# State-exchange attention feeding a gated two-layer network on one core: x first, the first layer's first step in plain float32, a new TensorE order in batch 0, and batch 1's second softmax moved behind it

## The chip, the core and the metric

The kernel runs on one core of one Trainium2 chip. The metric is the device time of one execution in microseconds (us), the median of the runs. TensorE (PE) multiplies matrices into PSUM, VectorE (DVE) and ScalarE (ACT) work element by element, SyncE (SP) issues most of the DMA transfers, and GpSimd (POOL) does almost nothing here. TensorE's weight loads are shown by the profile as an engine of their own, PEld.

## The reference

There are 8 batches `b` of 8 heads, 512 tokens and 32 states of 64 numbers. Token scores are turned into two softmaxes, one over the states for every token and one over the tokens for every state:

```python
scores = scale * x @ state.T          # a  = softmax over the 32 states
xread  = a @ state                    # 512 tokens read from the states
scores2 = scale * state @ x.T         # a2 = softmax over the 512 tokens
sread  = a2 @ x                       # 32 states read from the tokens
y = concat([xread, sread])            # 544 rows per head; heads side by side: 512 columns
h = y @ w_in                          # 512 -> 2048
g = where(h >= 1, h, where(h <= -1, 0, (h + 1)**2 / 4))
out = g @ w_out                       # 2048 -> 512
```

The weights come in as float64. They reach the kernel as pairs of 32-bit words, 1 MB for each of 16 chunks: 8 of `w_in` (256 of the 2048 columns each) and 8 of `w_out`.

## The kernel before

**The products.** The kernel doesn't form `xread`. It multiplies the states with each chunk of `w_in` (`sw_product`, L403, the tile `sw`) and then the softmax with that, which gives `h` directly (`Hidden.product`, L464). A number is split into a float32r part that is rounded (`...h`) and the rest (`...l`), and a product is three float32r matmuls: high by high, low by high, high by low (L478 to L480, and L538 to L540 for the second layer, `g2`). The scores, `sw`, the transposes on TensorE (`e2p`, `rt`) and the read of the states (`sr`) are plain float32.

**A step.** For each batch and each `j` of 0 to 7 there is one step of layer one (`g1`: two banks `h` of 128x512, 12 float32r matmuls), then the gate (`relu`, `square` on ACT, `bound` on DVE), the split of its result into `gh` (ACT, L500) and `gl` (DVE, L505), and one step of layer two (`g2`: 24 float32r matmuls into four banks `acc`). A bank `h` is read by `relu` and once more by `bound`, and is free after that. There are two banks `h`, four `acc`, and one pair of banks for transient results, `mm`, which `sw`, `e2p`, `sr`, `rt` and the scores of batches 1 to 7 share in turn. Batch 8 holds the state rows of all batches.

**Batch 0.** While batch 0 is computed the weights arrive and are made from their words: `high` (ACT, L592), `low` (ACT L584 or DVE L579), `join` (DVE, L600, into `w32` for `w_in`, into `wf` for `w_out`), and for `w_out` the split `part_high` (ACT, L607) and `part_low` (DVE, L611). The raw words of `w_in` have two buffers; SP issues the load of chunk `c + 2` when `w32` of chunk `c` is joined, and loads that stand behind it in SP's queue wait too.

**What sets the order.** All of batch 0 is recorded as operations with an engine, a cost, what they need and which buffers they take (`Plan`, L23). On TensorE and SP the order is that in which they are recorded; on DVE and ACT a list schedule puts the operation with the longest tail first, shifted by the numbers in `BIAS`. `emit` also fills TensorE's planned idle time before the first `g2` with multiplications of an identity matrix (`warm`, L195, tile `warmed`), whose results nobody reads. From batch 1 on the order is written out (`attention`, L803, and the loop at L840).

**Names.** `turn`, `top1`, `less1`, `exp1`, `sum1`, `inv1`, `norm1`, `back`, `high1`, `rest` make the first softmax `z`, its transpose `zt` and the split `ath`, `atl`. `top2`, `exp2` make the second softmax `e2`; `turn2` and `keep_turned` transpose it on TensorE and copy it back, or `turn_blocks` (DVE) and `shuffle` (16 DMAs on SP) do so without TensorE; `read2`, `scale2`, `keep2`, `keep` make the rows `srT`.

Of the kernel before, what the change touches and what calls it, by code (L numbers as in the profile page):

```python
# [17 lines left out]
WARM = 10  # L18
PAD = 120
BIAS = {('square', 0, 7): 4.9, ('high', 'o', 5): 4.6, ('wol', 7): -5.5, ('back', 0, 1): 2.8, ('atl', 1, 0): -6.5, ('w', 1): -2.8, ('swh', 0, 4): 4.5, ('wol', 5): 9.6, ('top2', 1, 1): 2.5, ('woh', 5): 4.1, ('swl', 1, 0): -0.5, ('swl', 0, 7): 2.1, ('gh', 0, 7): 0.6, ('low', 'i', 0): 2.6, ('wol', 6): 4.0, ('back', 1, 0): -2.1, ('turn', 0, 0, 1): -8.6, ('bound', 1, 0, 0): 3.3, ('high', 'o', 0): -4.3}  # L20
# [117 lines left out]
def state_exchange_moe(  # L138
# [68 lines left out]
    wo = {}  # L207
# [17 lines left out]
    class Attention:  # L225
# [60 lines left out]
        def inv1(self, q):  # L286
            _, _, s = self.parts(q)
# [14 lines left out]
        def high1(self, q):  # L302
            nc.scalar.copy(out=self.ath[:, q], in_=self.zt[:, q])
# [99 lines left out]
    def sw_product(b, c, n, apart=False):  # L403

        if apart:
            banks = [ps_h(f"sw{b}_{c}_{hh}") for hh in range(2)]
# [11 lines left out]
        w = n * CI  # L418
        wh, wl = (
# [36 lines left out]
    class Hidden:  # L456


        def __init__(self, b, j):
            self.b, self.j = b, j  # L460
            self.u = work.tile([P, 2, S], F32, tag="u", bufs=1, name=f"u{b}_{j}")
# [20 lines left out]

        def relu(self, i):
# [12 lines left out]
        def high(self):  # L496
# [3 lines left out]
            nc.scalar.copy(out=gh, in_=self.u)  # L500
# [18 lines left out]
    def g2(b, j, half=None):  # L519
# [12 lines left out]
        for i, t in pairs:  # L532
# [3 lines left out]
            lh, ll = (v[:, i // per, c0:c0 + P] for v in (gh, gl))  # L536
            a = acc[b][t]
            nc.tensor.matmul(a, lhsT=lh, rhs=oh, start=f == 0, stop=False)  # L538
# [55 lines left out]
    def join(kind, c):  # L594
# [3 lines left out]
        else:  # L598
            a = parts[c] = work.tile([P, 1024], F32, tag="tmp", name=f"wf{c}")
# [5 lines left out]
    def part_high(c):  # L605
        wo[c] = wop.tile([P, 2, 2, DM], F32R, tag="wo", name=f"wo{c}")
        nc.scalar.copy(out=wo[c][:, 0].rearrange("p a c -> p (a c)"), in_=parts[c])  # L607
# [17 lines left out]
    def chunk_ops(c):  # L625
# [24 lines left out]
    def att_ops1(b):  # L650
        def m(name, *a):
            return lambda: getattr(atts[b], name)(*a)

        for q in range(2):
# [14 lines left out]
            op(("inv1",) + k, "DVE", 0.4, m("inv1", q), [("sum1",) + k])  # L669
            op(("norm1",) + k, "DVE", 0.62, m("norm1", q), [("inv1",) + k])  # L670
        for q in range(2):
# [3 lines left out]
            op(("ath",) + k, "ACT", 0.52, m("high1", q), [("back",) + k], ends=[("zt", b)])  # L675
            op(("atl",) + k, "DVE", 0.62, m("rest", q), [("ath",) + k], ends=[("zt", b)])

    def att_ops2(b):
        def m(name, *a):
            return lambda: getattr(atts[b], name)(*a)  # L680

        for q in range(2):
            k = (b, q)
            take = [("tmp" if b == 0 else "e2", ("e2", b))] if q == 0 else []
            op(("top2",) + k, "DVE", 0.75, m("top2", q), [("sc", b) if b else ("sc", b, 1)] + [("top2", b, 0)] * q, take=take)
            op(("exp2",) + k, "ACT", 0.66, m("exp2", q), [("top2",) + k], ends=[("sc", b)])
        op(("kept", b), "ACT", 0.95, m("keep_turned"), [("e2p", b)], ends=[("e2p", b)])
# [3 lines left out]
    hid = {}  # L691

    def hidden_ops(b, j):
        k = (b, j)
        for i in range(2):
            op(("relu", i) + k, "ACT", 0.58, lambda i=i: hid[k].relu(i), [("p", i) + k], ends=[("h", i) + k],
               take=[("u", ("u",) + k)] if i == 0 else [])
# [3 lines left out]
        op(("gh",) + k, "ACT", 0.97, lambda: hid[k].high(), [("bound", 0) + k, ("bound", 1) + k],  # L701
# [6 lines left out]
    def product(i, b, j):  # L708
        if i == 0:
            hid[b, j] = Hidden(b, j)  # L710
        hid[b, j].product(i)

    def sw_ops(b, c, n):
        tensor(("sw", b, c), 0.35 + 0.35 * n, lambda: sw_product(b, c, n), [("w", c + i) for i in range(n)],
# [188 lines left out]
```

## Time and profile before

| | |
|---|---|
| time, median of 3 runs | 655.29 us (654.06 to 3663.21) |
| time of the profiled execution | 655.34 us |
| its span, first to last instruction | 653.6 us |
| PE busy | 644.3 us, 99% of the span |
| DVE busy, ACT busy | 354.7 us (54%), 371.5 us (57%) |
| mean granted TensorE clock | 0.997 |
| DMA | 46.80 MB, 72 GB/s over the span |
| second `h` step of batch 0 starts | 27.94 us |
| first `h` step of batch 1 starts | 99.60 us |

The time of an execution is 1.7 us more than its span. A row of the trace's timeline gives the start, the busy time, engine, line, operation, `out<-in`, the shape and how many instructions were merged; in brackets stands the idle time before it and what ended it. Busy times of neighbours overlap a little, so how long an instruction holds its engine is read from start to start.

### The profile page before, as it was taken

The numbers are of one execution on the slowest core, as the hardware profiler recorded it, in microseconds if no ns is written. First come the engines' busy times: TensorE is split into PE (matmuls) and PEld (weight loads), VectorE is DVE, ScalarE is ACT, GpSimd is POOL, SyncE is SP. The second block draws the span as 40 slices with busy tenths as digits, with TensorE's granted clock in tenths as the row PEclk, the third lists the DMA queues.
The fourth block names the chain that finished last, engine by engine and source line by source line (L and its number), as shares of the span: only waits on it lengthen the run. The fifth ranks groups of instructions, "written<-read, shape, count | busy, mean of one in ns | idle before, by whom it ended". The sixth has DMA issues, their size and how long they took to land.

```text
span 653.6 us, 10398 instructions
## 1 busy us (share of the span) xinstructions
PE 644.3 (99%) x4396; PEld 514.7 (79%) x4396; DVE 354.7 (54%) x514; ACT 371.5 (57%) x529; POOL 0.8 (0%) x7
## 2 busy tenths in 40 slices
PE   7999999999999999999999999999999999999997
PEld 6777777788777877787877877787877878788896
DVE  4999954564446643664456534664356543335531
ACT  4899856554546545655645555555545464545641
POOL 0000000000000000000000000000000000000000
PEclk9899999999999999999999999999999999999999
DMA  8897201032101401041101401031102001000101
GB/s 351 342 396 294 66 1 64 1 73 90 49 18 20 143 1 64 2 97 66 65 1 29 133 1 64 10 89 65 65 0 35 1 5 61 2 1 0 65 1 32
DMA packets 37198, 46.80 MB, mean 72 GB/s; under 512 B 27424, under 2 KB 27552, under 8 KB 34080
## 3 DMA queue, kind: packets, MB, share of 16 engines
q1 hardware_dynamic: 36672, 45.30, 20.1%
q10 hardware_dynamic: 480, 0.85, 0.4%
q8 instruction: 34, 0.56, 0.4%
q14 instruction: 12, 0.10, 0.1%
HBM read 34.08 MB, written 8.91 MB: 66 GB/s over the span
## 4 chain that ended last, share of the span: by engine, by line
PE 92%; ACT 4%; DVE 2%; DMA 1%; issue 0%; ACTq 0%; SPq 0%
PE acc L538 19%; PE acc L539 18%; PE acc L540 18%; PE h L478 10%; PE h L480 10%; PE h L479 10%; PE sw L414 4%; DMA xt<-in_xt_dram 1%; PE sr L369 1%; PE sc L253 1%; PE warmed L198 1%; ACT u L484 1%; ACT raw_i L592 1%; ACT gh L500 0%; ACT raw_o L592 0%; ACT u L488 0%
## 5 line engine op out<-in xcount | busy, mean ns | idle before, releaser
L538 PE MATMUL acc<-wo,gh 128*128 128x512 f32 x544 | 214.9, 395 | 0.0
L539 PE MATMUL acc<-wo,gh 128*128 128x512 f32 x544 | 212.2, 390 | 0.0
L540 PE MATMUL acc<-wo,gl 128*128 128x512 f32 x544 | 211.8, 389 | 0.0
L491 DVE SCALAR_TENSOR_TENSOR u<-u,h 128x512 f32<-128x512 f32 x136 | 92.8, 687 | 191.5 <-ACT u L488 191.5
L484 ACT ACTIVATE u<-h,half 128x512 f32<-128x512 f32 x136 | 93.7, 690 | 154.9 <-PE h L480 153.8
L538 PEld LDWEIGHTS acc<-wo,gh 128*128 128x128 f32 x544 | 102.1, 188 | 29.9 <-issue 8.7
L505 DVE TENSOR_TENSOR gl<-u,gh 128x1024 fp32r<-128x1024 f32 x68 | 83.2, 1224 | 68.2 <-ACT gh L500 68.1
L540 PEld LDWEIGHTS acc<-wo,gl 128*128 128x128 f32 x544 | 102.1, 188 | 21.8
L539 PEld LDWEIGHTS acc<-wo,gh 128*128 128x128 f32 x544 | 102.2, 188 | 20.4
L500 ACT CAST gh<-u 128x1024 fp32r<-128x1024 f32 x68 | 71.4, 1050 | 47.6 <-DVE u L491 47.6
L488 ACT ACTIVATE u<-u 128x512 f32<-128x512 f32 (+1 forms) x128 | 84.5, 660 | 3.8
L414 PE MATMUL sw<-w,sb 64*32 64x256 f32 x1024 | 33.1, 381 | 2.2 <-DVE w L600 2.2
L414 PEld LDWEIGHTS sw<-w,sb 64*32 64x32 f32 x1024 | 17.7, 106 | 14.3 <-issue 6.7
L478 PE MATMUL h<-ath,sw_6h 128*128 128x512 f32 x60 | 24.6, 410 | 0.0
L553 ACT COPY o<-acc 128x512 f32<-128x512 f32 x33 | 18.0, 587 | 10.9 <-PE acc L540 10.9
L478 PE MATMUL h<-ath,sw_2h 128*128 128x512 f32 x60 | 24.1, 402 | 0.0
L478 PE MATMUL h<-ath,sw_0h 128*128 128x512 f32 x60 | 23.6, 393 | 0.0
L480 PE MATMUL h<-atl,sw_2h 128*128 128x512 f32 x60 | 23.4, 391 | 0.0
L479 PE MATMUL h<-ath,sw_6l 128*128 128x512 f32 x60 | 23.4, 390 | 0.0
L480 PE MATMUL h<-atl,sw_6h 128*128 128x512 f32 x60 | 23.4, 390 | 0.0
L479 PE MATMUL h<-ath,sw_0l 128*128 128x512 f32 x60 | 23.4, 389 | 0.0
L480 PE MATMUL h<-atl,sw_0h 128*128 128x512 f32 x60 | 23.4, 389 | 0.0
(176 smaller groups left out, 726.3 us busy)
## 6 DMA issues: line engine op xcount, KB each, us to landing
raw_i<-in_moe_w_in_dram SPq DMA_DIRECT2D x8, 1024.0 KB, 6.3
raw_o<-in_moe_w_out_dram SPq DMA_DIRECT2D x8, 1024.0 KB, 8.7
xn<-in_x_dram SPq DMA_DIRECT2D x8, 1024.0 KB, 5.2
out_dram<-o SPq DMA_DIRECT2D x32, 256.0 KB, 2.2
xt<-in_xt_dram SPq DMA_DIRECT2D x15, 512.0 KB, 4.7
e<-eb SPq DMA_DIRECT2D x96, 32.0 KB, 1.9
xt<-in_xt_dram ACTq DMA_DIRECT2D x1, 512.0 KB, 7.6
sb<-in_state_dram SPq DMA_DIRECT2D x1, 448.0 KB, 11.8
```

What stands on the lines that cost most here:

```text
L414: nc.tensor.matmul(banks[hh][pr * NS:(pr + 1) * NS, i * CI:(i + 1) * CI], lhsT=sb[rows, b, pr], rhs=w32[c + i][rows, pr], start=True, stop ...
L478: nc.tensor.matmul(o, lhsT=wh[:, k, sl], rhs=ah[:, k], start=first, stop=False)
L479: nc.tensor.matmul(o, lhsT=wl[:, k, sl], rhs=ah[:, k], start=False, stop=False)
L480: nc.tensor.matmul(o, lhsT=wh[:, k, sl], rhs=al[:, k], start=False, stop=last)
L484: nc.scalar.activation(out=self.u[:, i], in_=self.hs[i], func=AF.Relu, scale=0.5, bias=half)
L488: nc.scalar.activation(out=u, in_=u, func=AF.Square)
L491: nc.vector.scalar_tensor_tensor(out=self.u[:, i], in0=self.u[:, i], scalar=1.0, in1=self.hs[i], op0=ALU.min, op1=ALU.max,)
L500: nc.scalar.copy(out=gh, in_=self.u)
L505: nc.vector.tensor_tensor(out=gl, in0=self.u, in1=gh.bitcast(F32), op=ALU.subtract)
L538: nc.tensor.matmul(a, lhsT=lh, rhs=oh, start=f == 0, stop=False)
L539: nc.tensor.matmul(a, lhsT=lh, rhs=ol, start=False, stop=False)
L540: nc.tensor.matmul(a, lhsT=ll, rhs=oh, start=False, stop=f == NF - 1)
```

## The change

- **Loads.** Both halves of batch 0's `x` are issued by SP, ahead of the weights; before, ACT issued the second half. ACT loads its function table with a one-element `Exp` at the start.
- **First scores.** Batch 0's scores go into the pair of banks `mm` instead of two banks `acc`. `sw` of chunks 0 and 1 goes into banks `acc` (the letter `a` in `ORDER`).
- **First step of layer one.** With `NH = 1`, step 0 of batch 0 isn't split: `sw` of chunk 0 is copied whole (`wh`, float32), and `product_part` multiplies it with the whole `zt`: four plain float32 matmuls of 128x512 in place of twelve float32r ones. `NG = 0`, so the code for a layer two in plain float32 (`part_late`, the branches on `NG`) is not used.
- **TensorE's order in batch 0** is written as words in `ORDER`. `sw3.2` and `sw5.2` make two chunks at once. The halves of `g2` stand in another order.
- **Batch 1's second softmax** is transposed by DVE and DMAs, as in later batches, and its `read2`, `scale2`, `keep2` and `keep` stand in batch 1, after its steps 1 and 3. The load of `xn` for batch 2 goes behind them.
- **Smaller things.** `inv1` is done for both halves at once; `WARM` is 6, not 10; the planner has other costs, other numbers in `BIAS`, and a table `ENG` that puts some copies on DVE and some `low` on ACT.

```diff
-WARM = 10
+WARM = 6
+NH = 1
+NG = 0
+ENG = {('low', 'o', 1): 'ACT', ('low', 'o', 2): 'ACT', ('woh', 5): 'DVE', ('low', 'o', 5): 'DVE', ('ath', 0, 0): 'DVE', ('low', 'i', 5): 'ACT', ('low', 'o', 3): 'ACT', ('woh', 3): 'DVE'}
+ORDER = "sw0.1a h0 sw1.1a e2p h1 sw2.1 g0.0 sr h2 g0.1 sw3.2 g1.0 h3 sc1 g2.1 g2.0 rt h4 g1.1 sw5.2 g3.1 g3.0 h5 sw7.1 g4.0 h6 g4.1 g5.1 h7 g5.0 g6.0 g6.1"
...
-            (nc.scalar if i and b == 0 else nc.sync).dma_start(out=xt[:, i], in_=xt_in[b, i])
+            nc.sync.dma_start(out=xt[:, i], in_=xt_in[b, i])
...
-                if b:
-                    sc = ps_mm(f"sc{b}")
-                    self.sc = [sc[:, hh] for hh in range(2)]
-                else:
-                    self.sc = [ps_acc(f"sc{b}_{hh}") for hh in range(2)]
+                sc = ps_mm(f"sc{b}")
+                self.sc = [sc[:, hh] for hh in range(2)]
...
-    def sw_product(b, c, n, apart=False):
+    def sw_product(b, c, n, apart=None):
...
-            banks = [ps_h(f"sw{b}_{c}_{hh}") for hh in range(2)]
+            banks = [apart(f"sw{b}_{c}_{hh}") for hh in range(2)]
...
+        if b == 0 and c < NH:
+            whole = work.tile([P, 1024], F32, tag="wh", name=f"sw{b}_{c}w").rearrange("p (q f) -> p q f", q=2)[:, :, :w]
+            sw_of[b, c] = [(banks[q][:, :w], whole[:, q], None) for q in range(2)]
+            chunk[b, c] = whole, None
+            return
...
+        def product_part(self, k):
+
+            j = self.j
+            if k == 0:
+                self.hs = [ps_h(f"h0_{j}_{i}") for i in range(2)]
+            w, _ = chunk[0, j]
+            for i in range(2):
+                nc.tensor.matmul(
+                    self.hs[i], lhsT=w[:, k, i * P:(i + 1) * P], rhs=atts[0].zt[:, k], start=k == 0, stop=k == 1
+                )
...
+        if b:
+            for q in range(2):
+                op(("blocks", b, q), "DVE", 0.62, m("turn_blocks", q), [("exp2", b, q)] + [("blocks", b, 0)] * q,
+                   take=[("tmp", ("eb", b))] if q == 0 else [])
+            return
...
     nc.scalar.dma_start(out=sb[:, 0], in_=state[:, 0])
+    nc.scalar.activation(out=small.tile([P, 1], F32, name="tabled"), in_=half, func=AF.Exp)
...
+    read(("eb", 1), 2.0, lambda: atts[1].shuffle(), after=[("blocks", 1, 0), ("blocks", 1, 1)])
...
+    for name in ("read2", "scale2"):
+        later("mid", 1, 1, (lambda name=name: getattr(atts[1], name)(),))
+    later("mid", 1, 1, (load_later, 2))
+    for name in ("keep2", "keep"):
+        later("mid", 1, 3, (lambda name=name: getattr(atts[1], name)(),))
```

The order of the instructions shows two places. The first is VectorE in batch 0, from the second transpose `back` of the first softmax to the first `bound` of step 0. Before (`z`, `zt` the softmax, `wf_247` and `wo_260` chunk 0 of `w_out`, `raw_i_178` and `raw_o_223` the words of chunk 2 of `w_in` and chunk 1 of `w_out`):

```order
L300 STREAM_TRANSPOSE zt_176<-z_117 128x512
L306 TENSOR_TENSOR atl_114<-zt_176,ath_113 128x512
L436 TENSOR_TENSOR sw_0l<-sw_0_205,sw_0h 128x512
L306 TENSOR_TENSOR atl_114<-zt_176,ath_113 128x512
L600 SCALAR_TENSOR_TENSOR w_1_88<-raw_i_128 128x1024
L600 SCALAR_TENSOR_TENSOR wf_247<-raw_o_145 128x1024
L579 TENSOR_SCALAR raw_i_178<-raw_i_178 128x1024
L611 TENSOR_TENSOR wo_260<-wf_247,wo_260 128x1024
L436 TENSOR_TENSOR sw_1l<-sw_1_263,sw_1h 128x512
L579 TENSOR_SCALAR raw_o_223<-raw_o_223 128x1024
L491 SCALAR_TENSOR_TENSOR u_0_239<-u_0_239,h_0_1_252 128x512
```

The same stretch of VectorE in the changed kernel (`wf_248` is chunk 0 of `w_out`, `raw_i_197` the words of chunk 2 of `w_in`):

```order
L301 STREAM_TRANSPOSE zt_205<-z_114 128x512
L318 TENSOR_REDUCE nm_0_193<-sc_113 128x1
L319 TENSOR_SCALAR nm_0_193<-nm_0_193 128x1
L662 CAST ath_111<-zt_205 128x512
L307 TENSOR_TENSOR atl_112<-zt_205,ath_111 128x512 x2
L627 SCALAR_TENSOR_TENSOR wf_248<-raw_o_142 128x1024
L602 TENSOR_SCALAR raw_i_197<-raw_i_197 128x1024
L441 TENSOR_TENSOR sw_1l<-sw_1_0_235,sw_1h 128x256
L441 TENSOR_TENSOR sw_1l<-sw_1_1_236,sw_1h 128x256
L511 SCALAR_TENSOR_TENSOR u_0_214<-u_0_214,h_0_0_215 128x512
```

The rest of `sw` of chunk 0, the split of chunk 0 of `w_out` (L611 before) and the `low` of chunk 1 of `w_out` have left the stretch. One cast of `ath` has come in, and the join of `w_1` and the second `top2` (L318, L319) have changed sides: the join now stands ahead of the second `back`, `top2` behind it. Further up, one `low` (chunk 0 of `w_in`) has come to VectorE from ScalarE.

The second place is TensorE from the end of step 0 to the start of step 1 of layer one. Before:

```order
L480 MATMUL h_0_1_252<-atl_114,sw_0h 128x512
L414 MATMUL sw_1_263<-w_1_88,sb 32x256 x8
L198 MATMUL warmed<-ident 128x128 x4
L333 MATMUL e2p_285<-ident,e_0_153 128x128 x8
L198 MATMUL warmed<-ident 128x128
L478 MATMUL h_1_0_304<-ath_113,sw_1h 128x512
L479 MATMUL h_1_0_304<-ath_113,sw_1l 128x512
L480 MATMUL h_1_0_304<-atl_114,sw_1h 128x512
```

The same in the changed kernel, from the last two of the eight multiplications of `sw_1`:

```order
L414 MATMUL sw_1_0_235<-w_1_88,sb 32x256
L414 MATMUL sw_1_1_236<-w_1_88,sb 32x256
L333 MATMUL e2p_250<-ident,e_0_192 128x128 x8
L202 MATMUL warmed<-ident 128x128 x6
L487 MATMUL h_1_0_277<-ath_111,sw_1h 128x512
L488 MATMUL h_1_0_277<-ath_111,sw_1l 128x512
L489 MATMUL h_1_0_277<-atl_112,sw_1h 128x512
```

`sw_1` has two tiles of its own, in banks `acc`, so `e2p` no longer takes the banks that `sw_1` had, and the multiplications by the identity stand behind `e2p`.

More of the change, by code (lines that the diff above doesn't have):

```diff
@@ L494, in bound, with high @@
             )
-        def high(self):
+        def high(self, engine="ACT"):
             b, j = self.b, self.j
@@ L535, in g2 @@
             c0 = (i % per) * n + t * P
-            lh, ll = (v[:, i // per, c0:c0 + P] for v in (gh, gl))
+            lh, ll = (v if v is None else v[:, i // per, c0:c0 + P] for v in (gh, gl))
             a = acc[b][t]
+            if ll is None:
+                nc.tensor.matmul(a, lhsT=lh, rhs=ol, start=f == 0, stop=False)
+                continue
             nc.tensor.matmul(a, lhsT=lh, rhs=oh, start=f == 0, stop=False)
@@ L691, in state_exchange_moe @@
     hid = {}
+    made = {}
     def hidden_ops(b, j):
         k = (b, j)
+        whole = b == 0 and j < NG
         for i in range(2):
-            op(("relu", i) + k, "ACT", 0.58, lambda i=i: hid[k].relu(i), [("p", i) + k], ends=[("h", i) + k],
-               take=[("u", ("u",) + k)] if i == 0 else [])
+            op(("relu", i) + k, "ACT", 0.58, lambda i=i: hid[k].relu(i), [("p", 1 if j < NH else i) + k], ends=[("h", i) + k],
+               take=[(("g", ("g",) + k) if whole else ("u", ("u",) + k))] if i == 0 else [])
         op(("square",) + k, "ACT", 0.97, lambda: hid[k].square(), [("relu", 0) + k, ("relu", 1) + k])
@@ L710, in product, with sw_ops @@
             hid[b, j] = Hidden(b, j)
[L711 to L716 removed]
+        if b == 0 and j < NH:
+            hid[b, j].product_part(i)
+        else:
+            hid[b, j].product(i)
+    def sw_ops(b, c, n, kind=""):
+        for i in range(n):
+            made[b, c + i] = c
+        tensor(("sw", b, c), 0.35 + 0.35 * n, lambda: sw_product(b, c, n, ps_acc if kind else None),
+               [("w", c + i) for i in range(n)],
+               take=[("acc" if kind else "mm", ("sw", b, c)), ("w", ("wc", b, c))])
+        flex(("swh", b, c), "ACT", (0.5 * n, 0.6 * n), lambda e: sw_high(b, c, e), [("sw", b, c)], ends=[("sw", b, c)])
+        if b == 0 and c < NH:
+            return
         op(("swl", b, c), "DVE", 0.6 * n, lambda: sw_low(b, c), [("swh", b, c)], ends=[("sw", b, c)])
@@ L720, in g1_ops @@
         for i in range(2):
-            need = [(x, b, j) for x in ("swh", "swl")] + [(x, b, q) for x in ("ath", "atl") for q in range(2)]
+            if j < NH:
+                need = [("swh", b, j), ("back", b, i)]
+                tensor(("p", i, b, j), 1.75, lambda i=i: product(i, b, j), need,
+                       take=[("h", ("h", x, b, j)) for x in range(2)] if i == 0 else [], ends=[("wc", b, j), ("zt", b)])
+                continue
+            need = [(x, b, made[b, j]) for x in ("swh", "swl")] + [(x, b, q) for x in ("ath", "atl") for q in range(2)]
             tensor(("p", i, b, j), 1.4, lambda i=i: product(i, b, j), need, take=[("h", ("h", i, b, j))],
-                   ends=[("wc", b, j)])
+                   ends=[("wc", b, made[b, j])])
     def g2_ops(b, j, half):
         k = (b, j)
-        tensor(("g2", half) + k, 2.75, lambda: g2(b, j, half), [("gh",) + k, ("gl",) + k, ("wol", j), ("sc done", 0)],
+        need = [("bound", 0) + k, ("bound", 1) + k, ("join", j)] + [(x, 0, c) for x, c in (("swh", 0), ("swh", 1), ("swl", 1)) if (x, 0, c) in plan.ops] if j < NG else [("gh",) + k, ("gl",) + k, ("wol", j)]
+        tensor(("g2", half) + k, 3.5 if j < NG else 2.75, lambda: g2(b, j, half), need,
                ends=[("g",) + k])
@@ L772, in state_exchange_moe @@
[L772 to L785 removed]
+        "e2p": lambda: tensor(("e2p", 0), 0.9, lambda: atts[0].turn2(), [("exp2", 0, 0), ("exp2", 0, 1)],
+                              take=[("mm", ("e2p", 0))]),
@@ new lines, in state_exchange_moe @@
+        "sr": lambda: tensor(("sr", 0), 1.1, lambda: atts[0].read2(), [("kept", 0), ("dma", "xn", 0)],
+                             take=[("mm", ("sr", 0))], ends=[("e2", 0), ("xn", 0)]),
+        "sc1": lambda: tensor(("sc", 1), 1.1, lambda: att_start(1), [("dma", "sb", 1), ("dma", "xt", 1)],
+                              take=[("mm", ("sc", 1))], ends=[("xt", 1)]),
+        "rt": lambda: tensor(("rt", 0), 0.3, lambda: atts[0].keep2(), [("rs", 0)], take=[("mm", ("rt", 0))]),
+    }
+    for word in ORDER.split():
+        if word in between:
+            between[word]()
+            if word == "sc1":
+                att_ops1(1)
+                att_ops2(1)
+        elif word[0] == "s":
+            c, n = word[2:].split(".")
+            sw_ops(0, int(c), int(n[0]), n[1:])
+        elif word[0] == "h":
+            g1_ops(0, int(word[1]))
+            hidden_ops(0, int(word[1]))
+        else:
+            g2_ops(0, int(word[1]), int(word[3]))
@@ L830, in state_exchange_moe @@
     later("end", 1, 0, (sw_make, 1, (2,)))
+    for c in range(NG):
+        later("mid", 1, 0, (part_late, c))
     later("mid", B - 1, 6, (states_split,))
```

127 lines of the change are left out of this document (65 added, 62 removed).

## The prediction

> **What bounds the kernel now.** I read the page first, then busy time by stretches, then TensorE's waits.
>
> ```profile
> PE 644.3 (99%) x4396; PEld 514.7 (79%) x4396; DVE 354.7 (54%) x514; ACT 371.5 (57%) x529; POOL 0.8 (0%) x7
> ```
>
> ```profile
> 0.00:31.50 31.50, 26.40 (x212) 21.42 (x212) 22.12 (x43) 20.14 (x26) 0.83 (x7) 0.95 0.88 353
> 31.50:100.00 68.50, 68.36 (x528) 51.30 (x521) 58.06 (x79) 55.54 (x71) 0.00 (x0) 1.00 0.47 184
> 100.00:200.00 100.00, 100.00 (x658) 78.70 (x658) 52.27 (x77) 56.56 (x86) 0.00 (x0) 1.00 0.15 48
> ```
>
> ```profile
> PE sw L414 <- DVE w L600: 2.2, 1, 2.2
> PE sc L253 <- DMA xt<-in_xt_dram: 1.0, 1, 1.0
> PE e2p L333 <- DVE sw_1l L436: 0.5, 1, 0.5
> ```
>
> The columns of the stretches are length, then busy time of PE, PEld, DVE, ACT, POOL, the clock, DMA share and GB/s. TensorE is never idle from 31.5 us on, and its only idle spells lie ahead of that. So the time is the moment at which TensorE begins gapless work, plus that work. What TensorE does before is in the timeline of its first 28 us:
>
> ```profile
> 1.45 4.63 PE L198 MATMUL warmed<-ident 128*128 128x128 f32 x20 [1.45 <-POOL ident masks.py:199]
> 6.01 1.11 PE L253 MATMUL sc<-xt,sb 64*32 64x256 f32 x16
> 8.93 0.67 PE L253 MATMUL sc<-xt,sb 64*32 64x256 f32 x16 [0.97 <-DMA xt<-in_xt_dram]
> 9.53 5.62 PE L198 MATMUL warmed<-ident 128*128 128x128 f32 x48
> 17.32 0.78 PE L414 MATMUL sw<-w,sb 64*32 64x256 f32 x16 [2.16 <-DVE w L600]
> 18.03 3.75 PE L198 MATMUL warmed<-ident 128*128 128x128 f32 x18
> 26.75 1.09 PE L333 MATMUL e2p<-ident,e 128*128 128x128 f32 x8 [0.52 <-DVE sw_1l L436]
> 27.94 0.50 PE L478 MATMUL h<-ath,sw_1h 128*128 128x512 f32 x1
> ```
>
> Most of it is multiplication of the identity, which is filler. From step 1 of layer one, at 27.94, all is real work. The change can gain at this front end, and where it takes instructions off TensorE; 2% of the time is 13.1 us, about what a measurement of this kernel tells from no change, and the front end holds hardly that much.
>
> **The front end.** VectorE sets it. Its rows:
>
> ```profile
> 9.72 0.78 DVE L260 STREAM_TRANSPOSE z<-sc 128x256 f32<-128x256 f32 x2 [1.10 <-PE sc L253]
> 19.76 0.68 DVE L436 TENSOR_TENSOR sw_0l<-sw,sw_0h 128x512 fp32r<-128x512 f32 x1
> 24.86 1.22 DVE L611 TENSOR_TENSOR wo<-wf,wo 128x1024 fp32r<-128x1024 f32 x1 [0.95 <-ACT wo L607]
> 26.61 0.69 DVE L579 TENSOR_SCALAR raw_o<-raw_o 128x1024 int32<-128x1024 uint32 x1
> 27.21 0.68 DVE L491 SCALAR_TENSOR_TENSOR u<-u,h 128x512 f32<-128x512 f32 x1
> ```
>
> From the second half of the scores (9.72) to the first `bound` (27.21 + 0.68 = 27.89) VectorE has 18.17 us with one real gap. The bound frees the bank that step 1 takes at 27.94.
>
> Where that stretch starts depends on `x`:
>
> ```profile
> xt<-in_xt_dram SPq DMA_DIRECT2D x1, 512.0 KB, 3.8
> xt<-in_xt_dram ACTq DMA_DIRECT2D x1, 512.0 KB, 7.6
> raw_i<-in_moe_w_in_dram SPq DMA_DIRECT2D x1, 1024.0 KB, 7.1
> ```
>
> The first half takes 3.8 us to land, the second, issued by ACT beside 1 MB of weights, 7.6, and lands no sooner than they do. Issued by SP ahead of the weights I expect it some 1.3 us behind the first (half of 1 MB, at the 353 GB/s of the first stretch or a little above): at 6 us, not 8.8. The scores of the first half can then start at 4.5: six multiplications of the identity give 12 records at 4.63/20 = 0.23, so the filler ends at 4.25. Scores take 1.11, the two fillers behind them 0.92 (4 x 0.23), the second half starts at 6.5 to 7.0, and VectorE's stretch at 8.0 (bounds 7.75 and 8.4).
>
> The stretch itself loses `sw_0l` (0.60 by the next row's start, 0.68 by its own), the split of chunk 0 of `w_out` with the gap ahead of it (0.95 + 1.15) and one `low` (26.61 to 27.21: 0.60): 3.3. It gains a `low` (0.60) and a cast of 128x512. No such cast on VectorE is in the trace; the nearest row has twice the size:
>
> ```profile
> L824 DVE CAST sath<-srT x1: 686/686/686, 590.0 to 590.0; 128x1024 fp32r<-128x1024 f32 x1
> ```
>
> So between 0.35 and 0.69; I take 0.4, since the row's form is the same and its size double. The stretch becomes 18.17 - 3.3 + 1.0 = 15.9, and step 1 starts at 8.0 + 15.9 + 0.05 = 23.95. **That is 4.0 us sooner** (3.3 to 4.5).
>
> What must stay hidden for that: the plain float32 step. Its four matmuls of 512 columns cost, by the filler at full clock (48 records of 128 columns in 5.62, two to a matmul: 0.234 per 128 columns), 4 x 4 x 0.234 = 3.75; at the least they cost as much as twelve float32r ones shrunk to four (0.9). I take 3.75, the row of the same type. They need `zt` alone. Between its first half and the end of that `bound` VectorE has two joins (1.2 each, like L611), `back`, `top2`, two `atl`, the `low` and the `bound` (0.6 to 0.7 each, like the rows of 128x512 and L579), the cast (0.4) and `sw_1l` (0.65): 7.3 or 7.4 us, so the first half is there at about 16.5 and the step ends at 20.3. Then come `sw_1` (0.6), `e2p` (0.9) and six fillers (1.4): 23.2, 0.75 ahead of VectorE. On ScalarE behind them come two `relu`, the copies of `sw_1` and `square`, done just before VectorE reaches `bound` at 23.3: that cover is only about 0.25. `e2p` doesn't wait for `sw_1l` any more. The table load at the start of ACT, the planner's costs and the merged `inv1` (shorter by some tenths) I count as nothing: ACT waits there for words from DMA.
>
> **From step 1 to batch 1.**
>
> ```profile
> 60.92 0.66 PE L414 MATMUL sw<-w,sb 64*32 64x256 f32 x16
> 61.51 0.50 PE L538 MATMUL acc<-wo,gh 128*128 128x512 f32 x1
> 68.08 0.39 PE L478 MATMUL h<-ath,sw_5h 128*128 128x512 f32 x1
> 71.48 0.50 PE L538 MATMUL acc<-wo,gh 128*128 128x512 f32 x1
> 78.32 0.39 PE L478 MATMUL h<-ath,sw_6h 128*128 128x512 f32 x1
> 90.20 0.39 PE L538 MATMUL acc<-wo,gh 128*128 128x512 f32 x1
> 95.73 1.09 PE L414 MATMUL sw<-w,sb 64*32 64x256 f32 x32
> 99.60 0.39 PE L478 MATMUL h<-ath,sw_0h 128*128 128x512 f32 x1
> ```
>
> These are starts of groups. A `g2` with nothing in it takes 95.73 - 90.20 = 5.53; with batch 1's `e2p` in it 68.08 - 61.51 = 6.57, with its `sr` 78.32 - 71.48 = 6.84. Both leave batch 0: 1.04 + 1.31. Two pairs of `sw` are made at once, 2 x 0.66 - 1.09 = 0.23 each: 0.46. Together 2.81 off TensorE.
>
> Against that stand new waits, for TensorE is ahead of the element-wise engines there. The first `g2` needs the split of chunk 0 of `w_out`, which left the stretch above. After `square` (by 23.3) ScalarE has `high`, `e2` kept, `gh` and `woh`, four passes over 1024 columns:
>
> ```profile
> L500 ACT CAST gh<-u 128x1024 fp32r<-128x1024 f32 x68 | 71.4, 1050 | 47.6 <-DVE u L491 47.6
> ```
>
> At about 1.0 to 1.05 each they end at 27.4, and `wol` (1.2) at 28.6. TensorE has a step and one `sw` to do until then, 71.48 - 68.08 = 3.40, and arrives at 27.35: a wait of 1.2. Two shorter ones I put at 0.5 together, for step 2 (its bank needs `bound`, now behind a `join`) and step 3 (its `sw`, two chunks in one pass). 1.7 in all; bounds are 0 (before has none) and 3.0.
>
> **Batch 1** takes over `sr` and `rt`:
>
> ```profile
> 150.60 1.10 PE L369 MATMUL sr<-xn,e 128*32 128x64 f32 x64
> 159.92 0.27 PE L383 MATMUL rt<-ident,rs 128*128 128x128 f32 x1
> ```
>
> That is 1.37 on the path, since nothing there is idle. The 16 DMAs of the shuffle stand in SP's queue ahead of batch 2's `x` and the stores; SP is held for them until VectorE has transposed, near 75 us, and neither is needed before 95. The extra transposes on VectorE lie where TensorE doesn't wait for it.
>
> **The sum,** against the profiled execution (655.34, the span 653.6 and 1.7 around it; the median is 655.29, so no correction): -4.0 - 2.81 + 1.7 + 1.37 = -3.7, or **651.6 us**. Its own range goes from 649.4 (lead 4.5, no waits) to 653.6 (lead 3.3, waits of 3.0).
>
> **Rivals.** (1) *The element-wise engines bound batch 0.*
>
> ```profile
> 60.00:70.00 10.00, 10.00 (x62) 7.64 (x61) 9.97 (x15) 10.00 (x13) 0.00 (x0) 1.00 0.51 211
> 70.00:76.00 6.00, 6.00 (x99) 4.23 (x98) 6.00 (x8) 5.83 (x9) 0.00 (x0) 1.00 0.00 0
> ```
>
> DVE and ACT are full here, and if they can't move forward TensorE waits for them at each later step until it is where it was. The lead and the 2.81 are returned, `sr` and `rt` still have to be done in batch 1: 655.34 + 1.37 = 656.7, **slower than before**. It decides once the waits after step 1 reach 6.8 us in place of 1.7. For it: VectorE gets some tenths more work there (two transposes, two casts). Against it: TensorE doesn't wait once in this stretch now, and the two engines start it some 4 us sooner too. 0.13.
>
> (2) *The clock falls at the front end.*
>
> ```profile
> 18.00:19.00 1.00, 1.00 (x11) 0.50 0.89 131
> 21.50:22.00 0.50, 0.50 (x5) 1.00 1.18 492
> ```
>
> Now TensorE is idle for 2.16 us ahead of 17.32, and right after it the granted clock is 0.50 for about 3 us; that costs nothing, for filler runs there. The change has gaps of about 1.3 us ahead of `sw_0` and 0.9 ahead of the plain step. If these bring half clock too, it lies on the plain step: 3.4 us at half cost 1.7, cover 0.25, so 651.6 + 1.45 = 653.1. 0.13, for the gaps are shorter.
> The Trainium skill ("TensorE: Matmul & The Clock Gate", section "What's actually happening") says that half clock comes after at least one idle window of about 3.4 us. By that rule the change's gaps are too short and the sum stays 651.6. The trace doesn't agree in full: the 2.16 us were enough.
>
> (3) *The second half of x lands no sooner.* Then the stretch starts at 9.72 and step 1 at 25.67, the lead is 2.27 and the time 653.3. Against it stands the first half's 3.8 us. 0.05.
>
> (4) *No new waits.* VectorE and ScalarE run further ahead than I think: 649.9. 0.10.
>
> **The numbers.** The forecast has 0.57, the rivals 0.13, 0.13, 0.05 and 0.10; 0.02 is for what I don't see. 649.2 to 654.8 takes in the forecast's own range and rivals 2 to 4 and leaves out the first. All cases lie within 2%: 0.97; faster 0.01, since that would take halving the front end; slower 0.02.
>
> **What would show it.** Second-half scores near 7 us and VectorE's next row near 8; step 1 near 24; one wait of TensorE of about 1 us ahead of the first `acc`, and under 1 us after it; batch 1's first step near 94.6. Step 1 after 25 makes the front end wrong; batch 1's first step at 97 or later is rival 1; a granted clock of 0.50 between 16 and 20 us with step 1 later is rival 2.

## The result and the profile after

The changed kernel takes 650.36 us (median of 4 runs, 649.98 to 650.64); its time is 0.9925 of the time before, with a 95% interval of 0.9913 to 0.9937. One of the four runs of before took 3663.21 us and is left out of its median. The forecast was 651.6. The profiled execution took 650.61 us, its span is 648.8 us, and the mean granted clock is 1.000: 4.73 us less than the profiled execution of before, where 3.7 less had been worked out.

The page's busy times, and then the two stretches in which before was read (length, busy time of PE, PEld, DVE, ACT and POOL, the clock, DMA share, GB/s):

```profile
PE 640.5 (99%) x4360; PEld 510.1 (79%) x4360; DVE 356.1 (55%) x500; ACT 369.5 (57%) x527; POOL 0.8 (0%) x7
```

```profile
0.00:31.50 31.50, 27.75 (x231) 19.69 (x235) 23.56 (x44) 22.32 (x32) 0.83 (x7) 1.00 0.94 385
31.50:100.00 68.50, 68.03 (x470) 51.89 (x459) 59.27 (x78) 55.98 (x69) 0.00 (x0) 1.00 0.46 169
```

The page has 36 instructions of TensorE fewer than before. The shape is as before: TensorE has work all the time from about 33 us on, but for one wait of 0.2 at 42.5, and what can be won lies ahead of that and in the number of its instructions. The clock of the first stretch is now 1.00 (0.95 before). TensorE's timeline up to step 1:

```profile
4.88 1.11 PE L254 MATMUL sc<-xt,sb 64*32 64x256 f32 x16 [0.50 <-DMA sb<-in_state_dram]
7.07 1.11 PE L254 MATMUL sc<-xt,sb 64*32 64x256 f32 x16
...
13.87 0.67 PE L414 MATMUL sw<-w,sb 64*32 64x256 f32 x16 [0.29 <-DVE w L627]
16.99 3.68 PE L499 MATMUL h<-zt,sw_0w 128*128 128x512 f32 x8 [0.92 <-DVE zt L301]
20.60 0.66 PE L414 MATMUL sw<-w,sb 64*32 64x256 f32 x16
...
23.93 0.50 PE L487 MATMUL h<-ath,sw_1h 128*128 128x512 f32 x1 [0.30 <-DVE u L511]
```

Step 1 starts at 23.93 (27.94 before). The second half of the scores no longer waits for `x`; among the DMA issues, both halves stand in one row (how many, KB each, median us to landing):

```profile
xt<-in_xt_dram SPq DMA_DIRECT2D x2, 512.0 KB, 4.3
```

What releases step 1 is still VectorE's `bound` (L511). VectorE's rows of the front end:

```profile
8.28 0.78 DVE L261 STREAM_TRANSPOSE z<-sc 128x256 f32<-128x256 f32 x2 [0.78 <-PE sc L254]
19.25 0.42 DVE L662 CAST ath<-zt 128x512 fp32r<-128x512 f32 x1
23.19 1.28 DVE L511 SCALAR_TENSOR_TENSOR u<-u,h 128x512 f32<-128x512 f32 x2
27.02 1.22 DVE L645 TENSOR_TENSOR wo<-wf,wo 128x1024 fp32r<-128x1024 f32 x1
```

Behind step 1 there are waits where before had almost none. TensorE's waits from step 1 to the end (total, times, longest; the first row is steps 1 and 2):

```profile
PE h L487 <- DVE u L511: 0.6, 2, 0.3
PE acc L562 <- DVE wo L645: 0.3, 1, 0.3
PE h L488 <- DVE sw_3l L441: 0.2, 1, 0.2
```

And where they lie behind step 1, with the groups on either side and batch 1's first step (step 3's wait, for `sw_3l`, lies at 42.51):

```profile
27.51 0.50 PE L561 MATMUL acc<-wo,gh 128*128 128x512 f32 x1
28.30 0.51 PE L562 MATMUL acc<-wo,gh 128*128 128x512 f32 x1 [0.29 <-DVE wo L645]
31.01 1.10 PE L369 MATMUL sr<-xn,e 128*32 128x64 f32 x64
32.43 0.50 PE L487 MATMUL h<-ath,sw_2h 128*128 128x512 f32 x1 [0.31 <-DVE u L511]
93.40 0.39 PE L487 MATMUL h<-ath,sw_0h 128*128 128x512 f32 x1
```

So the 4.8 us of the span come out like this. Step 1 is 4.01 sooner. From step 1 to batch 1's first step TensorE needs 93.40 - 23.93 = 69.47 in place of 71.66, which is 2.19 less. From there to the end of the span it needs 648.8 - 93.40 = 555.4 in place of 653.6 - 99.60 = 554.0, which is 1.4 more. Together -4.8.

### The profile page after: what moved, and what is told of

The parts are those of the page before. It is cut to its first block, busy times and chain, and to the rows that moved or that the text cites. A ratio compares the mean times of both kernels' runs of the same rounds, so it can differ in the third digit from the quotient of the medians.

```text
span 648.8 us, 10342 instructions
## 1 busy us (share of the span) xinstructions
PE 640.5 (99%) x4360; PEld 510.1 (79%) x4360; DVE 356.1 (55%) x500; ACT 369.5 (57%) x527; POOL 0.8 (0%) x7
## 4 chain that ended last, share of the span: by engine, by line
PE 93%; DVE 3%; ACT 2%; DMA 1%; issue 0%; SPq 0%
PE acc L561 19%; PE acc L562 19%; PE acc L563 18%; PE h L487 10%; PE h L488 10%; PE h L489 10%; PE sw L414 4%; PE sc L254 1%; PE sr L369 1%; DMA sb<-in_state_dram 1%; DVE u L511 0%; ACT u L504 0%; DVE w L627 0%; ACT gh L664 0%; ACT raw_o L615 0%
## 5 line engine op out<-in xcount | busy, mean ns | idle before, releaser
L511 DVE SCALAR_TENSOR_TENSOR u<-u,h 128x512 f32<-128x512 f32 x136 | 92.8, 687 | 186.0 <-ACT u L508 185.3
L488 PE MATMUL h<-ath,sw_2l 128*128 128x512 f32 x60 | 23.3, 389 | 0.0
L487 PE MATMUL h<-ath,sw_6h 128*128 128x512 f32 x56 | 23.1, 412 | 0.0
L487 PE MATMUL h<-ath,sw_0h 128*128 128x512 f32 x56 | 21.9, 391 | 0.0
L488 PE MATMUL h<-ath,sw_6l 128*128 128x512 f32 x56 | 21.9, 391 | 0.0
L489 PE MATMUL h<-atl,sw_6h 128*128 128x512 f32 x56 | 21.9, 390 | 0.0
L261 DVE STREAM_TRANSPOSE z<-sc 128x512 f32<-128x512 f32 (+1 forms) x18 | 10.9, 638 | 20.0 <-PE sc L254 19.8
```

Source lines behind the costliest of these rows:

```text
L487: nc.tensor.matmul(o, lhsT=wh[:, k, sl], rhs=ah[:, k], start=first, stop=False)
L488: nc.tensor.matmul(o, lhsT=wl[:, k, sl], rhs=ah[:, k], start=False, stop=False)
L489: nc.tensor.matmul(o, lhsT=wh[:, k, sl], rhs=al[:, k], start=False, stop=last)
L511: nc.vector.scalar_tensor_tensor(out=self.u[:, i], in0=self.u[:, i], scalar=1.0, in1=self.hs[i], op0=ALU.min, op1=ALU.max,)
```

## The experiments

The theory is that of the prediction: TensorE is the bound, the front end is a chain through VectorE that starts with the scores, and each part of the change is worth what it takes off that chain or off TensorE. The main rival is that the element-wise engines bound batch 0, so that work taken off TensorE comes back as waits. Each kernel below is the changed one with one part undone, but for the fifth, which is the kernel before with one part alone.

**`x` issued by ACT again.**

```diff
-            nc.sync.dma_start(out=xt[:, i], in_=xt_in[b, i])
+            (nc.scalar if i and b == 0 else nc.sync).dma_start(out=xt[:, i], in_=xt_in[b, i])
```

> The changed kernel with one part undone: ACT issues the second half of batch 0's x again, beside the weights. The order on all engines is unchanged but for that one DMA. Theory (VectorE's stretch from the second half of the scores to the first bound sets the front end): the second half lands near 8.8 us as before, its scores start at 8.9, VectorE's stretch starts at about 9.7 instead of 8.28 and keeps its length of 15.6, so step 1 of layer one starts at 25.3 instead of 23.93 and the time is 651.8 us (+1.4). Rival (TensorE's own front end, that is the plain float32 step, sw_1, e2p and the filler, which has 0.30 us of wait left, sets it, and the early x was only slack): step 1 stays at 23.9 to 24.2, the time at 650.4 to 650.7.

Measured: 652.06 us (651.47 to 652.16), 0.9951 of the kernel before (0.9935 to 0.9966). TensorE's timeline:

```profile
9.01 0.67 PE L254 MATMUL sc<-xt,sb 64*32 64x256 f32 x16 [2.09 <-DMA xt<-in_xt_dram]
18.48 3.68 PE L499 MATMUL h<-zt,sw_0w 128*128 128x512 f32 x8 [0.83 <-DVE zt L301]
25.42 0.50 PE L487 MATMUL h<-ath,sw_1h 128*128 128x512 f32 x1 [0.30 <-DVE u L511]
```

The scores start 1.94 later, but this half of them took 0.60 here and 1.04 in after (see the last section), so VectorE's stretch begins at 9.77, 1.49 later. The plain step is 1.49 later too, and so is step 1; batch 1 starts at 94.94, 1.54 later. The delay passes through VectorE to the end whole: the chain is as read. The front of it is worth 1.7 us in the medians.

**Step 0 split, as before.**

```diff
-NH = 1
+NH = 0
```

> The changed kernel with one part undone: step 0 of layer one is split again (twelve float32r matmuls, sw of chunk 0 in two parts). The list schedule is made anew. Theory (the plain step gains by what it doesn't have to wait for: the casts and rests of the softmax and sw_0l, not by its time on TensorE): step 0 starts after the second rest of the softmax, near 21.5 instead of 16.99, and though it takes 2.9 instead of 3.6 us the bound behind it is about 3.5 us later; step 1 starts near 27.5 and the time is 654 us (+3.5). Rival (only the sw_0l of 0.6 us on VectorE counts): step 1 at 24.6, time 651.0.

Measured: 657.15 us (656.94 to 658.18), 1.0033 of the kernel before (1.0021 to 1.0045). TensorE's timeline, the rows of `sw_1` behind step 0 and of step 1:

```profile
22.99 0.66 PE L414 MATMUL sw<-w,sb 64*32 64x256 f32 x16
27.49 0.50 PE L487 MATMUL h<-ath,sw_1h 128*128 128x512 f32 x1 [1.71 <-DVE u L511]
```

Step 1 starts at 27.49, as was worked out, but not all of the 3.56 us is the split's. Step 0 ends 2.39 later than in after (22.99 against 20.60). The other 1.2 lie behind it, where the order made anew differs: VectorE does a `join` and the split of chunk 0 of `w_out` (1.24 and 1.23) ahead of the first `bound`, and ScalarE does `woh` ahead of the second `relu`; in after all three stand behind. And the whole is some 3 us longer than expected. TensorE's waits:

```profile
PE h L487 <- DVE u L511: 3.1, 3, 1.7
PE h L488 <- DVE sw_3l L441: 1.2, 1, 1.2
PE h L489 <- DVE atl L307: 0.9, 1, 0.9
```

From step 1 to batch 1 it takes 100.03 - 27.49 = 72.54 where after takes 69.47: the waits go on behind step 1, for `bound` and for a copy of `sw`. VectorE has more to do for the split (`sw_0l`, and an `atl` that is due earlier), and is late with later work as well; that this is the whole reason is argued from the rows, and not shown. All other parts of the change are in this kernel, and it is slower than before.

**No filler between the scores and the first `g2`.**

```diff
-        plan.emit(warm, ("sc", 0, 0), ("g2", 0, 0, 0))
+        plan.emit(lambda n: None, ("sc", 0, 0), ("g2", 0, 0, 0))
```

This leaves out multiplications whose results nobody reads.

> The changed kernel without the planned multiplications of the identity between the first scores and the first step of layer two (the six at the very start stay). No order changes on DVE and ACT. Theory (the filler keeps the granted clock up; an idle spell of over 2 us brought 0.50 in the kernel before): TensorE idles from 8.1 to 13.9, the clock falls to 0.50 for about 3.4 us, some of it under the plain step of 3.6 us; that step ends 1 to 1.7 us later, and since the cover behind it is 0.3 us, step 1 starts at 24.6 to 25.3 and the time is 651.2 to 651.9. Rival (filler is worth nothing here): 650.4, with step 1 at 23.9.

Measured: 652.38 us (651.18 to 653.02), 0.9953 (0.9936 to 0.997). TensorE's timeline, then the granted clock in stretches of the same execution (the number ahead of the last two):

```profile
13.12 1.11 PE L414 MATMUL sw<-w,sb 64*32 64x256 f32 x16 [5.69 <-DVE w L627]
16.24 6.74 PE L499 MATMUL h<-zt,sw_0w 128*128 128x512 f32 x8 [2.02 <-DVE zt L301]
26.04 0.50 PE L487 MATMUL h<-ath,sw_1h 128*128 128x512 f32 x1 [1.44 <-DVE u L511]
```

```profile
13.00:18.00 5.00, 2.86 (x18) 1.06 (x19) 4.93 (x11) 3.98 (x8) 0.00 (x0) 0.50 1.02 404
18.00:22.00 4.00, 4.00 (x6) 1.69 (x5) 3.83 (x7) 1.51 (x4) 0.00 (x0) 0.50 1.00 416
22.00:23.00 1.00, 1.00 (x10) 0.09 (x16) 0.00 (x0) 0.43 (x1) 0.00 (x0) 0.79 1.02 414
```

The plain step takes 6.74 in place of 3.68. It began 0.75 sooner than in after, as VectorE's stretch did (7.53 against 8.28); from its start to step 1 it takes 9.80 us in place of 6.94, which is 2.9 more, and in the end step 1 is 2.1 later. This is the prediction's second rival, made to happen. In after it doesn't happen, since the filler leaves gaps of 0.29 and 0.92 only and the clock stays at 1.00. The half clock lasted longer than I had expected, through nearly the whole of the step and not part of it. This is shown for the profiled execution, the slowest of the five (653.02). The mean granted clocks of the five don't order their times (651.18 at 0.992, 652.78 at 0.999), so whether half clock is what the others lost too stays open.

**First scores in banks `acc`, as before.**

```diff
-                sc = ps_mm(f"sc{b}")
-                self.sc = [sc[:, hh] for hh in range(2)]
+                if b:
+                    sc = ps_mm(f"sc{b}")
+                    self.sc = [sc[:, hh] for hh in range(2)]
+                else:
+                    self.sc = [ps_acc(f"sc{b}_{hh}") for hh in range(2)]
...
-ORDER = "sw0.1a h0 sw1.1a e2p h1 ...
+ORDER = "sw0.1 h0 sw1.1 e2p h1 ...
```

> The changed kernel with one part undone: the first scores in two banks acc, sw of chunks 0 and 1 in the transient pair mm, as before. Theory (e2p then waits for the two sw_1l on VectorE, which end at 23.2, and takes 0.93; the filler stands ahead of it): step 1 starts at about 24.2, the time is 650.7 (+0.3). Rival (the banks are what freed the front end: before, step 1 followed sw_1l by 1.25 us): step 1 at 24.5 to 25.5, the time 651 to 652.

Measured: 650.33 us (649.92 to 650.62), 0.9926 (0.991 to 0.9941), the same as after. TensorE's timeline:

```profile
5.09 0.67 PE L257 MATMUL sc<-xt,sb 64*32 64x256 f32 x16 [0.71 <-DMA xt<-in_xt_dram]
22.43 1.09 PE L336 MATMUL e2p<-ident,e 128*128 128x128 f32 x8 [0.50 <-DVE sw_1l L444]
23.28 0.47 PE L490 MATMUL h<-ath,sw_1h 128*128 128x512 f32 x1
```

The wait of `e2p` for `sw_1l`, which the exchange of banks takes away, is back with 0.50. Step 1 follows it at once, where in after it waits 0.30 for `bound`: the later `e2p` fills that gap and a little more. From the start of the plain step (16.12) to step 1 it takes 7.16 us, in after 6.94, so the exchange gains 0.2 at step 1, near the 0.3 expected; that step 1 is sooner than in after comes from faster scores (last section). In the time the exchange is worth nothing that these runs can tell.

**The kernel before with both halves of `x` issued by SP, and nothing else.**

```diff
-            (nc.scalar if i and b == 0 else nc.sync).dma_start(out=xt[:, i], in_=xt_in[b, i])
+            nc.sync.dma_start(out=xt[:, i], in_=xt_in[b, i])
```

> The kernel before with one part of the change alone: SP issues both halves of batch 0's x ahead of the weights. All orders are as before but for that DMA. Theory (the early start of VectorE's stretch counts by itself): the second half of the scores is read at 8.3 instead of 9.72, step 1 of layer one starts at 26.5 instead of 27.94, the time is 654.0 us (-1.4). Rival (here ScalarE, which loads its table and makes the first words only when the weights land at 8.4, holds the softmax): step 1 stays at 27.5 to 27.9, the time at 655.0 to 655.4.

Measured: 654.22 us (653.53 to 655.40), 0.9982 (0.9972 to 0.9991). TensorE's timeline:

```profile
7.39 0.99 PE L253 MATMUL sc<-xt,sb 64*32 64x256 f32 x16
...
26.73 0.50 PE L478 MATMUL h<-ath,sw_1h 128*128 128x512 f32 x1
```

Step 1 starts 1.21 sooner than before and the time is about 1 us less, where 1.4 was expected of both. This part helps alone too.

**Batch 1's second softmax in batch 0 by TensorE again** (words for `e2p`, `sr` and `rt` of batch 1 in the order, the transposes on VectorE and the shuffle left out):

```diff
-ORDER = "... sw5.2 g3.1 g3.0 h5 sw7.1 g4.0 h6 g4.1 g5.1 h7 g5.0 g6.0 g6.1"
+ORDER = "... sw5.2 g3.1 e2q g3.0 h5 sw7.1 g4.0 sr1 h6 g4.1 g5.1 h7 rt1 g5.0 g6.0 g6.1"
...
-    read(("eb", 1), 2.0, lambda: atts[1].shuffle(), after=[("blocks", 1, 0), ("blocks", 1, 1)])
...
-    for name in ("read2", "scale2"):
-        later("mid", 1, 1, (lambda name=name: getattr(atts[1], name)(),))
```

> The changed kernel with one part undone: batch 1's second softmax is transposed by TensorE, read and turned back in batch 0, in the new order (the transposes between the halves of the second layer's step 3, the read after half of step 4, the last transpose after step 7). The list schedule is made anew with the same numbers. Theory: on TensorE batch 0 gets 1.04 + 1.31 + 0.2 us longer and batch 1 1.4 us shorter, so TensorE's own work is 1.2 us more; step 1 of layer one stays at 23.9 within 0.3; what is above 651.6 us is waits for VectorE and ScalarE, whose order was numbered for the other work, and the trace shows them as gaps. Rival (it is a saving of the element-wise engines in batch 0, not of TensorE): TensorE's pieces are as long as in the changed kernel and only waits are added.

Measured: 653.70 us (653.57 to 654.66), 0.998 (0.997 to 0.999). TensorE's timeline:

```profile
22.91 0.50 PE L487 MATMUL h<-ath,sw_1h 128*128 128x512 f32 x1 [0.29 <-DVE u L511]
62.68 1.09 PE L333 MATMUL e2p<-ident,e 128*128 128x128 f32 x8 [1.57 <-DVE sw_5l L441]
73.46 1.10 PE L369 MATMUL sr<-xn,e 128*32 128x64 f32 x64 [0.67 <-DVE sw_7l L441]
97.79 0.39 PE L487 MATMUL h<-ath,sw_0h 128*128 128x512 f32 x1
```

Step 1 to batch 1 takes 74.88 in place of 69.47, and from batch 1 to the end 554.0 in place of 555.4: net 4.0 us more of TensorE's time. In the profiled executions the kernel takes 3.0 us more (653.57 against 650.61), since the first scores ran faster in this one and step 1 started 1.0 sooner; more on that below. The products that are back account for about 2.5 of the 5.4: 0.84 for `e2p` and 1.03 for `sr` from start to start, and some 0.2 for each of the three places where they interrupt `acc` or `h`. The other 3 us are waits, 1.6 and 0.7 of them in the rows above: both products take the pair of banks `mm` from a `sw`, and stand still until VectorE has made the low part of that `sw`.

**The pairs of `sw` made one by one.**

```diff
-ORDER = "... sw3.2 g1.0 h3 sc1 g2.1 g2.0 rt h4 g1.1 sw5.2 g3.1 g3.0 h5 sw7.1 g4.0 h6 g4.1 ...
+ORDER = "... sw3.1 g1.0 h3 sw4.1 g2.1 sc1 g2.0 rt h4 g1.1 sw5.1 g3.1 g3.0 h5 sw6.1 g4.0 h6 sw7.1 g4.1 ...
```

> The changed kernel with one part undone: chunks 3 to 6 of sw made one at a time, ahead of steps 3 to 6 as before, which puts two more plain float32 groups between the float32r ones. The list schedule is made anew with the same numbers. Theory: four groups of 0.59 take the place of two of 1.02 (0.16 each) and each extra switch between float32r and plain float32 costs about 0.1, so TensorE has 0.5 us more work: 650.9 us if no waits are added; waits show as gaps. Rival (a switch costs nothing, the doubled pieces alone count): 650.7. The two are told apart by the lengths of the pieces in the trace, not by the time.

Measured: 657.03 us (656.59 to 658.40), 1.0031 (1.002 to 1.0043). One wait outweighs everything; from TensorE's waits:

```profile
PE rt L383 <- ACT e L322: 3.7, 1, 3.7
```

This run was meant to measure the two extra interruptions (a few tenths). It doesn't: with `sc1` and the `sw` at other places the list schedule of DVE and ACT came out otherwise, and `rt` waits 3.7 us for work that ScalarE does too late. Behind the wait the granted clock is 0.50 for 3.4 us, which costs some 1.5 more. Together that is the larger part of the 7.0 us that TensorE takes longer here from step 1 (23.26) to batch 1 (99.75). What the interruptions cost is read from the lengths of pieces instead (below). As a test of the pairs it stays inconclusive.

**No shifts of the list schedule.**

```diff
-BIAS = {('woh', 2): 1.5, ('wol', 3): 1.9, ...}
+BIAS = {}
```

> The changed kernel with an empty table BIAS: TensorE's order, the loads and all work are the same, only the list schedule of VectorE and ScalarE in batch 0 has no shifts. This tries how much of the result lies in the order of the element-wise engines (the first rival of the prediction: TensorE ahead of them only waits). Theory: VectorE does the split of chunk 0 of w_out ahead of the first bound, so step 1 starts 1.1 us later, near 25.0, while the first layer-two step has no wait of its own; later steps wait 2 to 5 us more in all; time 653 to 656 us. Rival (order on VectorE and ScalarE hardly matters, TensorE's order does it): step 1 within 0.5 of 23.93 and the time under 651.5.

Measured: 658.16 us (656.84 to 658.62), 1.0036 (1.0026 to 1.0047), above what I had expected. TensorE's timeline:

```profile
24.18 0.50 PE L487 MATMUL h<-ath,sw_1h 128*128 128x512 f32 x1 [0.56 <-DVE u L511]
45.52 0.79 PE L487 MATMUL h<-ath,sw_3h 128*128 128x512 f32 x1 [4.11 <-DVE u L511]
99.61 0.39 PE L487 MATMUL h<-ath,sw_0h 128*128 128x512 f32 x1
```

The granted clock behind the long wait, and what ScalarE and VectorE did shortly ahead of it:

```profile
46.00:48.50 2.50, 2.50 (x7) 1.92 (x7) 2.50 (x4) 2.50 (x3) 0.00 (x0) 0.50 0.81 334
```

```profile
38.24 0.69 ACT L504 ACTIVATE u<-h,half 128x512 f32<-128x512 f32 x1 [2.86 <-DVE gl L525]
41.05 1.22 DVE L627 SCALAR_TENSOR_TENSOR wf<-raw_o 128x1024 int32<-128x1024 int32 x1 [2.93 <-ACT raw_o L615]
```

TensorE has the same instructions here as in after but for filler. It reaches batch 1 at 99.61, where before reached it at 99.60: the lead of 3.8 us at step 1 and all the work taken off TensorE are gone. From step 1 on it takes 75.43 in place of 69.47, 6.0 more. Most of that are two waits for `bound`, 4.1 and 1.1 us, and the half clock that the longer one brings: 0.50 for 3.4 us, where a multiplication takes 0.43 in place of 0.23, some 1.6 in all; in return step 2 and the first `acc` don't wait. (The start of step 1 isn't to be held against 23.93: the scores ran faster here. Against 22.91, of the kernel with the softmax in batch 0, it is 1.3 later.) This is rival 1's outcome, slower than before. Its mechanism is another one, though. Rival 1 had VectorE and ScalarE full; here, as the rows show, each stands idle for almost 3 us and waits for the other, just before the long wait of TensorE begins (41.4). By these rows it is their order that is lost and not their capacity. The profiled execution was the fastest of the eight; where the others lose up to 1.8 us more is not shown.

## Why the prediction was right, and where its terms were off

**The front end** is right, in its sum and in its mechanism: VectorE has no gap of note from 8.28 to its first `bound`, and that `bound` releases step 1. Step 1 came at 23.93 (forecast 23.95). The cast on VectorE took 0.42 (taken as 0.4), the plain step 20.60 - 16.99 = 3.61 (taken as 3.75). Two small misses cancel: VectorE's stretch began at 8.28 and not 8.0, for the scores waited 0.50 for the small slice of the states, which ACT issues, and took 1.04 for each half; and it was 15.65 long and not 15.9. That the sum fits to 0.02 is luck: with faster scores, step 1 came at 22.91 in the kernel with the softmax in batch 0, whose front end is the same (last section). The cover of the plain step was as thin as forecast: `square` ended at 22.96, 0.23 ahead of the `bound` at 23.19. The two kernels on `x` confirm the chain: 1.2 to 1.5 us at step 1 each. Undoing the plain step makes step 0 end 2.4 later and step 1 start 3.56 later; the difference is order, as said there.

**"Together 2.81 off TensorE"** is the mis-sized term, and the larger part of the 1 us by which the forecast was too high. What went off was 3.6: 69.47 in place of 71.66, with waits of 1.38 to be added back (below). By starts of groups, before and after, `e2p` gave 0.85, `sr` 1.03, `rt` 0.08 and the pairs of `sw` 0.29. Most of the rest comes from interruptions: a plain float32 group between float32r ones costs about 0.2 beside its own length (shown below). Before has 13 such visits between step 1 and batch 1 and after has 8, so some 1.0 went with them. The prediction had this for `e2p` and `sr`, since it took the difference of whole `g2` steps, but not for the pairs, where it compared the busy times of the groups themselves (0.23 a pair, 0.16 from start to start), and it left `rt` out (87.48 - 81.73 = 5.75 for a `g2` with `rt`, against 5.53). Another 0.2 is a wait in before that the prediction hadn't seen when it said that before has none; TensorE's timeline of before, with the first and last of twelve `acc` multiplications ahead of `rt`:

```profile
52.02 0.50 PE L538 MATMUL acc<-wo,gh 128*128 128x512 f32 x1
52.36 0.39 PE L539 MATMUL acc<-wo,gh 128*128 128x512 f32 x1
52.59 0.40 PE L540 MATMUL acc<-wo,gl 128*128 128x512 f32 x1
...
54.66 0.39 PE L540 MATMUL acc<-wo,gl 128*128 128x512 f32 x1
55.19 0.33 PE L383 MATMUL rt<-ident,rs 128*128 128x128 f32 x1
```

The piece takes 3.17, and the same piece between two other plain groups 34.48 - 31.52 = 2.96. Some 0.1 of the 3.6 stays open.

**The new waits of 1.7** were 1.38, at the three places named. The first was 0.54 and not 1.2 (3.50 for the first half of `g2`, 2.96 for such a piece in before): TensorE came when the prediction said (27.51, forecast 27.35), but ScalarE was ahead of the forecast and `woh` was ready (at 26.79, forecast 27.4), so that only `wol` was late, at 27.02 + 1.22 = 28.24 and not 28.6. Step 2 waited 0.39 for its bank (32.43 - 31.01 = 1.42, `sr` alone 1.03) and step 3 0.45 for its `sw` (45.23 - 41.97 = 3.26 for the step, against 66.93 - 64.12 = 2.81 for step 5), together 0.84 where 0.5 was put.

**Batch 1** took 1.4 more (forecast 1.37).

**The rivals.** (1) did not occur in after, yet its outcome was closer than the trace of before let one think. That TensorE "doesn't wait once in this stretch" before was a poor argument against it: with the shifts set to nothing the same TensorE work waits 5.2 us for `bound` behind step 1, loses 1.6 to the clock, and the time is above before. What kept this away is the order on DVE and ACT, which the prediction took as given and did not price. (2) did not occur: the gaps were 0.29 and 0.92 where 1.3 and 0.9 had been expected, and the clock stayed at 1.00. Its mechanism is real, and dearer than forecast: 2.9 us from the plain step's start to step 1 when the filler is left out (forecast 1.45). (3) did not occur: the two halves took 4.3 us to land, as the median of both. (4) did not occur.

**The parts don't add up.** In the medians, undoing one part costs 1.7 (`x`), 6.8 (plain step), 3.3 (softmax) and 7.8 us (shifts), 0 for the banks, and the whole change gave 4.9. Each part that is undone also takes away the fit of the order on DVE and ACT, and this share can't be told apart from the part's own worth by these runs.

## What to carry to other kernels

Where one engine is busy from some moment to the end, work out a change as the moment at which that begins plus what comes off that engine afterwards, and take the second from starts of whole groups on both sides, interruptions included. Then ask who must deliver by the new, earlier dates: work taken off the busy engine is worth nothing if the others' order isn't moved with it, and undoing that order alone is the run that shows it. A wait of some 4 us also brought half clock for the next 3.4 us here, so it has to be priced with that. An experiment that changes an order changes the schedule of the other engines as well, so read from its trace which wait took the time before reading anything from the time.

## What the runs showed of the hardware that I had not expected

- **A break in a stream of float32r multiplications costs TensorE up to 0.2 us beside what breaks it.** In the rows of before above, the first float32r multiplication after `sw` holds TensorE for 0.34 (52.02 to 52.36) and the next one for 0.23. On the way out it is the last one: in after the last `acc` ahead of `sw` holds it for 0.32, and its neighbour for 0.23:

```profile
56.98 0.39 PE L562 MATMUL acc<-wo,gh 128*128 128x512 f32 x1
57.21 0.39 PE L563 MATMUL acc<-wo,gl 128*128 128x512 f32 x1
57.53 1.09 PE L414 MATMUL sw<-w,sb 64*32 64x256 f32 x32
```

  That is 0.11 and 0.09. Before the runs I had taken the change between plain float32 and float32r for the reason, and the rows speak against that. After a mere wait, with float32r on both sides, the first one is as long: 0.34 (28.30 to 28.64 in after). And ahead of the transposes `e2p` and `rt`, which are plain float32 too, the last one in before takes 0.25 and 0.23 (64.15 to 64.40, 84.37 to 84.60); the 0.09 stands only ahead of `sw`, `sr` and the scores. The reason stays open.

- **Half clock came in lengths of 3.4 us.** In slices of 0.05 us the granted clock is 0.50 from 17.74 to 21.16 in before, from 45.43 to 48.84 without shifts, from 55.86 to 59.27 with `sw` one by one, and for four times that, 8.78 to 22.43, without filler. In the last, TensorE worked without a gap from 16.24 on, so full clock came back only 6 us into busy work. By the Trainium skill ("TensorE: Matmul & The Clock Gate", section "What's actually happening") the clock returns after at least one busy window of about 3.4 us. The trace agrees if the windows follow one another from 8.78 on: the one that ends at 19.0 still begins with idle time, and the next is the first full one. A plan that counts 3.4 us from the first busy moment would have been wrong by some 2.5 here.

- **The first multiplications ran at little more than half their later rate, while the row of the first stretch shows a granted clock of 1.00,** and not in every execution. A half of the scores takes 1.04 in the profiled execution of after (4.88 to 5.92) and 0.60 in that of the kernel with the old banks (5.09 to 5.69), with the same instructions, and the granted clock reads 1.00 in both; the same section says that the moment at which the clock wakes varies from run to run. For that reason step 1 is at 23.28 there and at 22.91 with the softmax in batch 0, where both halves took the shorter time, and these two starts are not compared with 23.93 above. Whether it also explains that the runs of one kernel lie some 0.6 us apart (649.98 and 650.10 against 650.61 and 650.64) is likely but was not shown.
